# Higher array-use thresholds for side matmuls and zero matmuls, with new order seeds, in a fused transformer-block kernel

## The chip, the cores and the metric

The kernel runs on one core of a Trainium2 chip. The time is device microseconds (us) of one execution. The engines are PE (TensorE matmul; PEld is its weight load), DVE (VectorE), ACT (ScalarE), POOL (GpSimd) and SP (SyncE, which here only issues transfers). PEclk in the profile is the share of full TensorE clock that was granted.

## The reference

One transformer block in bf16: S = 2048 rows, D = 512, 32 heads of 16, hidden width 1376, conditioned by six vectors.

```python
mod = (_silu(c) @ w_mod).reshape(c.shape[0], 6, 1, -1)
sa, ca, ga, sb, cb, gb = ...
h = _layernorm(x) * (1 + ca) + sa
x = x + ga * _A_ref(h, A_wqkv, A_wo)      # softmax attention, 32 heads, Dh = 16
h = _layernorm(x) * (1 + cb) + sb
x = x + gb * _B_ref(h, B_w1, B_b1, B_w2, B_b2)   # gelu(h @ w1 + b1) @ w2 + b2
```

## The kernel before

**Work and tiles.** Attention is cut into 32 runs. A run is four heads for one block of 512 queries (in the last block eight heads for half of it), over 16 key tiles of 128 keys. Each key tile gives four units of 128 x 512 scores: four matmuls that each use 32 of the array's 128 rows (function `qk`, L837). A score unit becomes an exponential in one of two ways. On ACT a group of three or two units goes through Exp (tiles `st` to `pt`, L886). On DVE the four units of a tile are turned into integers that are the bits of an approximate exponential (`ax` to `ph`, L927), and four shifted copies are made (`sh`, L942). A run may give up to four of its 16 tiles to DVE (the first run one); what DVE doesn't get to, ACT takes back (`next_tile`). The product with the values is a group of four matmuls that use 32 columns each (`pv_op`, L975, into `od`); a DVE tile needs five such groups, an ACT tile one. There is one `od` bank, so run follows run. At the end of a run `normalise` copies `od` out and sends the denominators through DRAM on the SP queue, and POOL multiplies (L1027).

**Side work.** All other matmuls run beside attention: projections for queries, keys and values (L716, L755), and for each finished block of 512 rows `block_tail`: output projection (L1135), layer norm, the two MLP matmuls (L1202, L1141). They share the two `ax` PSUM banks with the DVE score units, and DVE evicts most of them. The queries' projections also send 8 small transfers each on the SP queue (`qm<-qs`). A side matmul has a due point, counted in score units done.

**The planner.** Nothing is written out by hand: class `Plan` runs an event model while the program is built, and emits the instructions in the order in which the model starts them. `pick` takes, on each engine, among operations that can start at nearly the same time, the one with the lowest cost (`dyn`, plus `spread`, a pseudo-random 0 to 0.15 made from the kind of the operation and a seed; there is one seed of `SEEDS` for each 25 us of planned time). The order is then fixed; the engines wait on semaphores.

**Array use.** `commit` keeps a list of the array time of the matmuls of the last 30 us (0.2155 us for a full one of 512 columns, a quarter of that for one score unit, `MM`), adds it up backwards, and finds two times, which lie WIN = 3.4 us behind the matmul at which the sum reaches HEAT or FILL. In words: `cool` is when the use of the last 3.4 us falls below HEAT, `fill_at` when it falls below FILL.

```python
            for t, us in reversed(self.done):
                tot += us
                if tot >= HEAT and not self.cool:
                    self.cool = t + WIN
                if tot >= self.fill:
                    self.fill_at = t + WIN
                    break
```

Three rules use them. A side matmul that isn't due yet (`later`) can't start before `fill_at` (`start`, L139). An attention group in `pv_op` that starts after `cool` is doubled: four more matmuls with a zero operand are added to the same bank (`o.extra`, L203, `zeros`, L461). And between operations of PE the planner puts in a single matmul with zeros after `cool` (`heat`, L441 to L455; into a free `ax` bank, L445, or the open `od`, L461) if it ends before the next PE operation can start, or if that is a DVE score unit. Until the first score group (`front`) these zero matmuls don't ask for `cool`.

Of the kernel before, what the change touches and what calls it, by code (L numbers as in the profile page):

```python
# [58 lines left out]
DL = 0.14  # L59
DPL = 0.08  # L60
AL = 0.055
FILL = 1.6
SPREAD = 0.15
SEEDS = (942, 880, 561, 237, 414, 526, 187, 975, 867, 591, 361, 470, 931, 275, 675, 561, 623, 980, 746, 5, 392, 802, 877, 840, 977, 907, 960, 53, 524, 828, 132, 531)
HEAT = 1.45


class Res:
# [38 lines left out]
class Plan:  # L107
    SLACK = {"NIL": 0.0, "PE": 0.10, "DVE": 0.05, "ACT": 0.15, "POOL": 0.05, "SP": 0.05}

    def __init__(self, dyn, later):  # L110
# [6 lines left out]
        self.dve = (0.0, 0.0, True)  # L117
        self.dyn, self.done, self.fill = dyn, deque(), FILL

# [39 lines left out]
    def spread(self, o):  # L159
        x = ((sum(map(ord, o.kind)) if o.eng == "PE" else o.fn.__code__.co_firstlineno if o.fn else 0) * 2654435761 ^ SEEDS[min(int(self.now // 25.0), len(SEEDS) - 1)] * 2246822519) & 0xFFFFFFFF  # L160
        x = ((x ^ x >> 15) * 2246822519) & 0xFFFFFFFF
        return SPREAD * ((x ^ x >> 13) & 1023) / 1024.0
# [33 lines left out]
    def commit(self, s, o):  # L196
# [11 lines left out]
        if o.eng == "PE":  # L208
# [5 lines left out]
# [4 lines that stand above are left out]
# [1250 lines left out]
```

## Time and profile before

| what | before |
|---|---|
| median of 3 runs | 786.5 us (785.47 to 789.52) |
| profiled execution: its time | 786.56 us |
| its span | 784.8 us |
| busy ACT / PE / DVE / POOL | 755.3 / 743.1 / 734.5 / 122.2 us |
| granted clock, mean | 0.995 |

The difference of 1.8 us between time and span lies around the program. Busy times are unions of an engine's instructions. A matmul's recorded duration holds its latency too (a lone group of four takes 0.39 to 0.40 us, two in a row 0.62), so a PE that is busy for 95% of the span isn't at 95% of its throughput. ACT is the busiest, and from 25 to 750 us it hardly pauses. The tables below cut the span into stretches; rows of groups give a line of the kernel, engine, operation, out<-in tiles, shape, count, busy time, mean duration in ns, and the idle time before them.

### The profile page before, as it was taken

What the parts mean: (1) busy time and instruction counts of PE and PEld (TensorE: products, weight loads), DVE (VectorE), ACT (ScalarE), POOL (GpSimd) and SP (SyncE); (2) the same over time, 40 slices, a digit from 0 to 9 for tenths busy, and PEclk for the clock granted to TensorE, in tenths of its full rate; (3) what the DMA queues carried; (4) which work ended last, traced back from release to release, by engine and by line L of the source; (5) the groups of instructions that cost most, each with busy time, mean ns of one, the idle gap of its engine ahead of it and who ended that gap; (6) DMA issues with size and microseconds to landing.
All of it is one profiled execution on the core that took longest, in us unless ns stands there. A gap on an engine that the chain in (4) does not pass through costs nothing.

```text
span 784.8 us, 20739 instructions
## 1 busy us (share of the span) xinstructions
PE 743.1 (95%) x8381; PEld 271.4 (35%) x8381; DVE 734.5 (94%) x1288; ACT 755.3 (96%) x680; POOL 122.2 (16%) x279
## 2 busy tenths in 40 slices
PE   8899999999999998999999999999998999999997
PEld 3433323333333222232223323222243444334445
DVE  6889899999999999999999999999798999999993
ACT  4999999999999999999999999999998999999993
POOL 6520304021122430010000100000000100010100
PEclk9999999999999999999999999999999999999999
DMA  7034011000002010000100110001100001000000
GB/s 215 32 96 129 19 23 47 22 17 20 16 19 71 22 52 18 17 16 22 47 9 20 31 27 26 12 17 30 59 26 18 22 20 46 18 23 18 26 18 28
DMA packets 38545, 27.70 MB, mean 35 GB/s; under 512 B 17941, under 2 KB 33846, under 8 KB 38450
## 3 DMA queue, kind: packets, MB, share of 16 engines
q1 hardware_dynamic: 38442, 26.39, 12.2%
q8 instruction: 65, 1.06, 0.6%
q14 instruction: 30, 0.25, 0.1%
q10 hardware_dynamic: 8, 0.00, 0.0%
HBM read 20.77 MB, written 2.61 MB: 30 GB/s over the span
## 4 chain that ended last, share of the span: by engine, by line
PE 24%; ACT 20%; DVE 13%; issue 5%; DMA 1%; SPq 0%; DVEq 0%; ACTq 0%
ACT pt L886 18%; PE od L975 8%; PE st L837 6%; DVE ph L927 6%; DVE sh L942 4%; PE ax L1141 3%; PE ax L1202 2%; PE ax L837 2%; DVE g L1207 1%; PE ax L716 1%; PE t L1312 1%; ACT g L1217 1%; DVE OD L1000 0%; DMA qm<-qs 0%; DMA dc<-dn 0%
## 5 line engine op out<-in xcount | busy, mean ns | idle before, releaser
L886 ACT ACTIVATE pt<-st 128x1536 bf16<-128x1536 f32 x629 | 714.2, 1312 | 6.0 <-PE st L837 3.8
L927 DVE TENSOR_SCALAR ph<-ax 128x512 int16<-128x512 f32 x476 | 309.8, 684 | 15.2 <-PE ax L837 13.5
L942 DVE TENSOR_SCALAR sh<-ph 128x2048 int16<-128x2048 int16 x476 | 310.1, 695 | 6.1 <-PE od L975 5.7
L837 PE MATMUL st<-qm,kT 32*128 32x512 bf16 x1572 | 247.3, 384 | 20.6 <-ACT pt L886 16.4
L837 PE MATMUL ax<-qm,kT 32*128 32x512 bf16 x476 | 162.1, 380 | 7.3 <-DVE ph L927 3.7
L975 PE MATMUL od<-sh,VX 128*32 128x512 bf16 (+1 forms) x2400 | 166.4, 341 | 2.8 <-DVE sh L942 1.9
L837 PEld LDWEIGHTS <-kT 32*128 32x128 bf16 x2048 | 79.7, 91 | 243.6 <-issue 232.5
L975 PE MATMUL od<-pt,VEB 128*32 128x512 bf16 (+1 forms) x1960 | 144.8, 341 | 0.4 <-ACT pt L886 0.4
L975 PEld LDWEIGHTS <-VEB 128*32 128x32 bf16 x2560 | 62.4, 96 | 72.8 <-issue 59.5
L975 PEld LDWEIGHTS <-VX 128*32 128x32 bf16 x2400 | 58.1, 95 | 84.7 <-issue 73.7
L1027 POOL TENSOR_TENSOR OT<-OD,RB 128x256 bf16<-128x256 f32 x38 | 27.0, 726 | 306.9 <-DVE sh L942 170.2
L975 PE MATMUL od<-ph,VEB 128*32 128x512 bf16 (+1 forms) x600 | 47.6, 338 | 0.7 <-DVE OD L1000 0.6
L1202 PE MATMUL ax<-blk,W 128*128 128x512 bf16 (+1 forms) x176 | 44.7, 356 | 0.6 <-DVE ph L927 0.4
L1027 POOL TENSOR_TENSOR OS<-OD,RB 128x256 bf16<-128x256 f32 x24 | 17.2, 727 | 139.8 <-DVE sh L942 68.3
L716 PE MATMUL ax<-blk,w 128*128 128x512 bf16 x124 | 37.4, 389 | 1.6 <-DVE ph L927 0.6
L1141 PE MATMUL ax<-w,g 128*128 128x512 bf16 x128 | 33.9, 381 | 1.5 <-ACT g L1212 1.0
L771 POOL TENSOR_SCALAR VX<-VEB 128x128 bf16<-128x128 bf16 x64 | 23.2, 362 | 71.7 <-DVE VEB L647 67.8
L1207 DVE TENSOR_SCALAR g<-ax,b1c 128x512 bf16<-128x512 f32 (+1 forms) x44 | 29.4, 678 | 0.1
L621 DVE BATCH_NORM_STATS2 ln_s<-xb 128x6 f32<-128x512 bf16 x32 | 21.7, 677 | 1.3 <-DMA xb<-in_A_x_dram 1.2
L1141 PEld LDWEIGHTS <-g 128*128 128x128 bf16 x176 | 14.2, 97 | 24.0 <-issue 11.1
L1202 PEld LDWEIGHTS <-W 128*128 128x128 bf16 x176 | 13.5, 97 | 23.3 <-issue 18.7
L1000 DVE COPY OD<-od 128x512 f32<-128x512 f32 x31 | 21.3, 686 | 0.1
(106 smaller groups left out, 374.2 us busy)
## 6 DMA issues: line engine op xcount, KB each, us to landing
RB<-rn SPq DMA_DIRECT2D x124, 64.0 KB, 2.1
xb<-in_A_x_dram SPq DMA_DIRECT2D x7, 512.0 KB
out_dram<-o SPq DMA_DIRECT2D x16, 128.0 KB
qm<-qs SPq DMA_DIRECT2D x120, 16.0 KB, 1.8
W<-in_B_w_dram SPq DMA_DIRECT2D x1, 1376.0 KB
w<-in_A_wqkv_dram SPq DMA_DIRECT2D x3, 384.0 KB
blk<-in_w_mod_dram SPq DMA_DIRECT2D x2, 512.0 KB
g<-in_w_mod_dram SPq DMA_DIRECT2D x2, 512.0 KB, 4.3
```

The lines of the kernel that those rows point to most:

```text
L621: nc.vector.bn_stats(out=st6, in_=src)
L716: return chain([(lambda ps, j=j: nc.tensor.matmul(out=ps[:, 0:QB], lhsT=w.tile[:, j, cc * P:(cc + 1) * P], rhs=o_h[b].tile[:, j, :], start ...
L771: nc.gpsimd.tensor_scalar(out=v_cols(VX[(t, ph)])[:, 8 * cc:8 * cc + 8, 0:16], in0=v_cols(v_tile(t, 0))[:, 8 * cc:8 * cc + 8, 0:16], scala ...
L837: nc.tensor.matmul(out=o.tile[:, k * QB:(k + 1) * QB], lhsT=kT[cc][kb][rows, ko * P:(ko + 1) * P], rhs=qm.tile[rows, par, :] if hb is None ...
L886: nc.scalar.activation(out=e.tile[:, 0:len(got) * QB], in_=o.tile[:, 0:len(got) * QB], func=ACT.Exp, scale=ESC)
L927: nc.vector.tensor_scalar(out=ph.tile[:, o.row * QB:(o.row + 1) * QB], in0=o.tile, scalar1=PH_B, scalar2=0.0, op0=ALU.add, op1=ALU.max)
L942: sh = op("DVE", lambda o, j=j: nc.vector.tensor_scalar(out=o.tile, in0=first.tile, scalar1=PH_SH[j], scalar2=None, op0=ALU.add), 0.6, es, ...
L975: nc.tensor.matmul(out=o_od[r].tile[32 * i:32 * i + 32, n * HB:n * HB + w], lhsT=v_tile(kt, ph)[:, c0:c0 + 32], rhs=got[i][:, at:at + w], ...
L1027: two = beside(lambda c: nc.gpsimd.tensor_tensor(out=OT.tile[:, c], in0=OD.tile[:, c], in1=o5.tile[:, c], op=ALU.mult), (OT,), (OD, o5), f ...
L1141: nc.tensor.matmul(out=ps, lhsT=g[:, f, col:col + P], rhs=rhs, start=(f == 0), stop=(f == NF - 1))
L1202: mm = chain([(lambda ps, f=f, j=j, f0=f0: nc.tensor.matmul(out=ps[:, (f - f0) * N:(f - f0 + 1) * N], lhsT=W1[:, j, f * P:(f + 1) * P], rh ...
L1207: ev.append(op("DVE", lambda o, f=f, f0=f0, mm=mm: nc.vector.tensor_scalar(out=g.tile[:, f, 0:N], in0=mm.tile[:, (f - f0) * N:(f - f0 + 1) ...
```

## The change

The two thresholds are raised, FILL from 1.6 to 2.1 and HEAT from 1.45 to 1.7 (us of array time per 3.4 us), and all 32 seeds are replaced. No operation of the block's mathematics changes, and no transfer is added or removed. What changes is the order that the planner emits on every engine, the moment at which side matmuls that aren't due may start, and the number and places of zero matmuls.

```diff
-FILL = 1.6
+FILL = 2.1
 SPREAD = 0.15
-SEEDS = (942, 880, 561, 237, 414, 526, 187, 975, 867, 591, 361, 470, 931, 275, 675, 561, 623, 980, 746, 5, 392, 802, 877, 840, 977, 907, 960, 53, 524, 828, 132, 531)
-HEAT = 1.45
+SEEDS = (189, 218, 297, 155, 171, 163, 261, 540, 974, 172, 672, 279, 663, 728, 301, 465, 719, 329, 508, 485, 116, 24, 319, 395, 351, 431, 815, 192, 264, 111, 379, 921)
+HEAT = 1.7
```

## The prediction

> **What bounds the kernel now.** I read the busy shares first, then the chain that ended last, then the groups, and last the span in stretches of 25 us and, where those looked odd, of 1 us. From the page of the profile:
>
> ```profile
> PE 743.1 (95%) x8381; PEld 271.4 (35%) x8381; DVE 734.5 (94%) x1288; ACT 755.3 (96%) x680; POOL 122.2 (16%) x279
> PE 24%; ACT 20%; DVE 13%; issue 5%; DMA 1%; SPq 0%; DVEq 0%; ACTq 0%
> L886 ACT ACTIVATE pt<-st 128x1536 bf16<-128x1536 f32 x629 | 714.2, 1312 | 6.0 <-PE st L837 3.8
> L927 DVE TENSOR_SCALAR ph<-ax 128x512 int16<-128x512 f32 x476 | 309.8, 684 | 15.2 <-PE ax L837 13.5
> L942 DVE TENSOR_SCALAR sh<-ph 128x2048 int16<-128x2048 int16 x476 | 310.1, 695 | 6.1 <-PE od L975 5.7
> L837 PE MATMUL st<-qm,kT 32*128 32x512 bf16 x1572 | 247.3, 384 | 20.6 <-ACT pt L886 16.4
> ```
>
> ACT, DVE and PE are balanced, and no one of them is the bound alone: the chain changes between them all the time. ACT and DVE share one pool of score tiles. 1572 units on ACT are 393 tiles at 714.2/393 = 1.82 us each; 476 on DVE are 119 tiles at (309.8 + 310.1)/119 = 5.21 us each. Both together do 1/1.82 + 1/5.21 = 0.741 tiles per us. So a microsecond lost on ACT moves the end by (1/1.82)/0.741 = 0.74 us, one lost on DVE by 0.26 us; these are my exchange rates. PE has some room: it waits 16.4 us for ACT to give a score bank back (last row).
>
> The stretches show where ACT doesn't run. Columns: stretch, length, busy time of PE, PEld, DVE, ACT, POOL, granted clock, DMA share, GB/s.
>
> ```profile
> 200.00:225.00 25.00, 24.33 (x248) 8.90 (x246) 23.72 (x41) 24.04 (x22) 5.02 (x11) 0.93 0.08 19
> 575.00:600.00 25.00, 22.57 (x341) 9.09 (x331) 21.21 (x36) 22.32 (x20) 1.40 (x2) 0.93 0.10 27
> ```
>
> ```profile
> 200.00:201.00 1.00, 0.76 (x4) 0.19 (x2) 1.00 (x3) 1.00 (x2) 0.41 (x1) 0.92 0.00 0
> 201.00:202.00 1.00, 1.00 (x5) 0.11 (x3) 1.00 (x3) 1.00 (x2) 0.00 (x0) 0.50 0.00 0
> 203.00:204.00 1.00, 1.00 (x7) 0.24 (x10) 0.13 (x1) 0.95 (x2) 0.00 (x0) 0.50 0.00 0
> 594.00:595.00 1.00, 1.00 (x16) 0.29 (x8) 1.00 (x2) 0.42 (x1) 0.00 (x0) 0.50 0.08 17
> ```
>
> Twice the granted clock falls to half for some 3.4 us, from 200.7 and from 593.3. These are the two stretches before 750 us in which ACT loses the most, 0.96 and 2.68 us; elsewhere it stands for hardly 2 us from 25 to 750.
>
> What PE did ahead of the first of them (timeline):
>
> ```profile
> 198.37 0.37 PE L837 MATMUL ax<-qm,kT 32*128 32x512 bf16 x1
> 199.28 0.40 PE L975 MATMUL od<-pt,VEB 128*32 128x512 bf16 x4
> 199.61 0.39 PE L837 MATMUL ax<-qm,kT 32*128 32x512 bf16 x1
> 199.87 0.39 PE L837 MATMUL st<-qm,kT 32*128 32x512 bf16 x2
> ```
>
> Between 197.4 and 200.7 there are only two attention groups and twelve score units: 2 x 0.2155 + 12 x 0.054 = 1.08 us of array time, while PE was never still for as much as 0.5 us. So in this trace a small sum of array time, not a pause, stands ahead of the half clock.
>
> [...]
>
> **The change, part by part.** The array time of attention alone comes from the groups, shapes kept apart:
>
> ```profile
> L837 PE MATMUL ax<-qm,kT 32*128 32x512 bf16 x476 | 162.1, 380 | 7.3 <-DVE ph L927 3.7 <-DMA qm<-qs 2.0 <-DVE g L1207 0.4
> L975 PE MATMUL od<-sh,VX 128*32 128x512 bf16 x1408 | 123.8, 387 | 2.4 <-DVE sh L942 1.5
> L975 PE MATMUL od<-pt,VEB 128*32 128x512 bf16 x1184 | 108.7, 384 | 0.4 <-ACT pt L886 0.4
> L975 PE MATMUL od<-ph,VEB 128*32 128x512 bf16 x352 | 35.4, 384 | 0.7 <-DVE OD L1000 0.6
> L461 PE MATMUL od<-warm 128*32 128x512 bf16 x208 | 19.2, 392 | 0.0
> L445 PE MATMUL ax<-warm 128*128 128x512 bf16 x24 | 9.5, 471 | 0.0
> ```
>
> Units: 2048 x 0.054 = 110 us. Groups: (1408 + 1184 + 352)/4 = 736 x 0.2155 = 159 us, and the last block's 2016 matmuls of half width another 54 us. Together 323 us over the 742 us from 20 to 762 us in which attention runs: 0.435, or 1.48 us per 3.4 us. So the old HEAT (1.45) lies just below what attention does by itself and the new one (1.7) above it. The side matmuls of that time come to some 114 us by their counts (128 + 132 + 176 + 62 of full width and 108 for the narrow ones by their share, less some 78 at both ends, x 0.2155), 0.52 us per 3.4 us. All work averages 2.0, so FILL at 2.1 lies above the mean: a side matmul that can run will nearly always be let through ahead of its due point.
>
> *Clock.* With more use demanded, the first half-clock stretch should go. Its cost: ACT's 0.96 us and DVE's 1.28 us in that stretch, 0.74 x 0.96 + 0.26 x 1.28 = 1.0 us. The second lies behind a stall from 589 to 592 us, in which PE waited for the query transfers (`qm<-qs`) behind the four `RB` issues on SP's queue; no threshold sees that. Its clock part costs 1.3 us (ACT 1.49, DVE 0.70 from 594 to 596). Bounds: 0 and -2.3. I take -1.0, the one that a low sum alone explains.
>
> *Zero matmuls.* If side work runs at 2.1 - 1.48 = 0.62 us per 3.4 us, its 114 us last 625 of the 742 us; the other 117 us have none. There HEAT asks for 1.7 - 1.48 = 0.22 us, about one group of zeros per 3.4 us: 117/3.4 = 34 groups beside the 52 + 24 that L461 and L445 show now, 7.4 us of PE. Two groups in a row last 0.62 us where one lasts 0.40, so 0.22 us each is right. Cover: PE's 16.4 us of waiting for score banks. Without cover a doubled group holds back the score units queued behind it on PE, and ACT and DVE wait for those. Bounds: 0 if all falls in that wait, 7.4 if none does. I take PE's share of the chain, 24%: +1.8.
>
> *Side work earlier.* It moves DVE's evictions forward too, at the same count. A run takes 742/32 = 23.2 us, four DVE tiles 20.8, so in a run without side work DVE has 2.4 us over that the limit of four tiles leaves unused, while ACT takes back tiles in crowded runs. 117 us are five such runs: 12 us of DVE, 3.1 us of the end. Starting the next run's tiles early softens this (the `sh` copies have four buffers). Against it, DVE is idle 9.8 us from 25 to 125 us, where earlier side work would fit and give back at most 2.5. Bounds: -2.5 and +3.1; I take +1.2, because the evictions that remain after 125 us outweigh those before. The queues: the 8 transfers for each query group go out earlier on SP, which can only move them away from the `RB` issues of a run's end or onto those of another; tail loads and stores find SP free for most of a run, and POOL is busy 16%. These I cost at nothing; SP is the cover, and the 589 us stall shows the price without it: ACT 1.19 and DVE 2.92 us, 1.6 us.
>
> *Seeds.* They reorder operations of nearly the same start. No row prices it. The nearest is the one mishap of this order, the stretch at 575 us: 0.74 x 2.68 + 0.26 x 3.79 = 3.0 us. Bounds: one such mishap less or more, -3.0 and +3.0 (its clock part is in the first term already). I take 0, since an order is only known to have such mishaps, not how many.
>
> The first 20 us don't ask for `cool`, and after 762 us PE is dense: no cost there.
>
> Sum: -1.0 + 1.8 + 1.2 + 0 = +2.0 us on the profiled execution's 786.56 us, 788.56; that one lies 0.06 us above the median of the three runs, so **788.5 us**.
>
> **The rivals.**
>
> *Faster.* Both half-clock stretches go, the query transfers leave early enough that the 589 us stall goes as well, zeros fall in PE's waits, and early side work fills half of DVE's early idle time: -2.3 - 1.6 - 1.3 = -5.2, 781.3 us. The deciding mechanism is the cover: it holds as long as added zeros stay within the 16.4 us in which PE waits for score banks anyway. For it: 7.4 is less than 16.4. Against: those waits are 57 short ones, and the long runs of low use are not where they are.
>
> *Clearly slower.* Zeros lie in PE's path and DVE's evictions bunch: +7.4 + 3.1 - 1.0 = +9.5, 796 us. For it: PE has the largest share of the chain, and DVE is at 24.5 to 25.0 of 25 us in most stretches from 125 to 550 us, so an eviction that comes early pushes a score tile away. It decides where more than some 20 groups are doubled in line.
>
> [...]
>
> *The order hardly differs in what it costs.* If due points and dependences, not `fill_at`, hold most side work back, everything stays within 1 us of 786.5. For it: tail chains wait for each other's evictions.
>
> **How the numbers follow.** The forecast has 0.40 (own range 785 to 792), faster 0.26, clearly slower 0.24, no gain in clock 0.05, no difference 0.05. A measurement of this kernel tells a change from none at about 0.5% (its runs spread 785.47 to 789.52), so the limits are 782.6 and 790.4. Faster keeps its 0.26; slower takes its 0.24 and 0.07 from the upper end of the forecast and the clock case; 0.43 stays between. The range reaches from the faster case with 1.3 us of luck in the seeds, 780, to the slower one, 797.
>
> **What the profile after would show.** The clock term: no stretch with a granted clock of 0.5 around a low sum of array time; if they remain while zeros rise, that step is wrong. Zeros: L461 and L445 with some 30 groups more, and the share of PE in the chain higher. Side work: fewer than 476 units in L927, and DVE idle late in a block. Seeds: other places where ACT stands. The prediction is wrong if ACT's idle time between 25 and 750 us falls below 2 us and L927 keeps its 476 (faster), or if the wait of `pt` L886 for PE rises above 6 us (slower).

## The result and the profile after

The changed kernel takes 783.2 us (median of 6 executions, 782.91 to 783.32); the kernel before, beside it, 787.49 us (785.47 to 789.52). The ratio is 0.9944 (95% interval 0.9925 to 0.9963), 0.6% faster. A second comparison gave 782.8 us and 0.9928 (0.9903 to 0.9952). The forecast was 788.5 us, 2.0 us slower than before; the measured time lies on the other side of the kernel before.

The page of the kernel after (busy shares; the chain that ended last; groups):

```profile
PE 746.6 (96%) x8617; PEld 273.2 (35%) x8617; DVE 737.4 (94%) x1288; ACT 755.3 (97%) x680; POOL 124.5 (16%) x279
PE 34%; DVE 28%; ACT 26%; issue 8%; DMA 2%; SPq 1%; POOL 1%; DVEq 0%; ACTq 0%
L886 ACT ACTIVATE pt<-st 128x1536 bf16<-128x1536 f32 x629 | 714.2, 1308 | 2.2 <-PE st L837 1.0
L927 DVE TENSOR_SCALAR ph<-ax 128x512 int16<-128x512 f32 x476 | 310.4, 682 | 8.0 <-PE ax L837 6.8
L942 DVE TENSOR_SCALAR sh<-ph 128x2048 int16<-128x2048 int16 x476 | 312.6, 694 | 2.1 <-PE od L975 0.9
L837 PE MATMUL st<-qm,kT 32*128 32x512 bf16 x1572 | 246.4, 383 | 16.0 <-ACT pt L886 12.4
L461 PE MATMUL od<-warm 128*32 128x512 bf16 x440 | 41.7, 381 | 0.0
```

ACT's Exp is the same work to a tenth of a microsecond (629 instructions, 714.2 us), and DVE has the same 476 score units, so no tile changed engines. What fell is idle time: ahead of Exp from 6.0 to 2.2 us, ahead of `ph` from 15.2 to 8.0, ahead of `sh` from 6.1 to 2.1. Zero matmuls in `od` rose from 208 to 440, so from 52 groups to 110.

The two stretches in which the kernel before lost the most, in the kernel after (columns as in the prediction: stretch, length, busy time of PE, PEld, DVE, ACT, POOL, granted clock, DMA share, GB/s):

```profile
200.00:225.00 25.00, 23.59 (x272) 8.92 (x264) 25.00 (x42) 25.00 (x23) 6.32 (x12) 1.00 0.10 32
575.00:600.00 25.00, 24.52 (x375) 10.41 (x375) 24.52 (x42) 24.97 (x23) 1.42 (x2) 1.00 0.16 48
```

The clock is full in both, ACT stands for 0.00 and 0.03 us where it stood for 0.96 and 2.68 us (24.04 and 22.32 us busy), and the mean clock of each of the six executions is 1.000 (0.995 in the profiled execution before).

From 25 to 750 us (the first row is the kernel before, the second the kernel after; same columns) ACT is idle for 1.9 us instead of 5.2, and DVE for 22.4 instead of 29.6:

```profile
25.00:750.00 725.00, 691.88 (x7846) 243.92 (x7842) 695.37 (x1200) 719.76 (x626) 103.16 (x207) 1.00 0.11 30
25.00:750.00 725.00, 699.10 (x8139) 247.69 (x8140) 702.63 (x1208) 723.12 (x630) 105.75 (x209) 1.00 0.12 31
```

The prediction had named this as its sign for the faster rival: ACT idle for less than 2 us between 25 and 750 us, with 476 units in L927.

### The profile page after: what moved, and what is told of

It is laid out like the page before. It is cut to its first block, busy times and chain, and to the rows that moved or that the text cites. A ratio compares the mean times of both kernels' runs of the same rounds, so it can differ in the third digit from the quotient of the medians.

```text
span 781.3 us, 21165 instructions
## 1 busy us (share of the span) xinstructions
PE 746.6 (96%) x8617; PEld 273.2 (35%) x8617; DVE 737.4 (94%) x1288; ACT 755.3 (97%) x680; POOL 124.5 (16%) x279
## 4 chain that ended last, share of the span: by engine, by line
PE 34%; DVE 28%; ACT 26%; issue 8%; DMA 2%; SPq 1%; POOL 1%; DVEq 0%; ACTq 0%
ACT pt L886 24%; DVE sh L942 11%; DVE ph L927 11%; PE od L975 11%; PE st L837 10%; PE ax L1141 3%; PE ax L837 3%; PE ax L716 2%; PE ax L1202 2%; PE od L461 1%; DVE OD L1000 1%; DVE ln_s L621 1%; PE ax L1135 1%; DMA xb<-in_A_x_dram 1%; PE ax L755 1%
## 5 line engine op out<-in xcount | busy, mean ns | idle before, releaser
L886 ACT ACTIVATE pt<-st 128x1536 bf16<-128x1536 f32 x629 | 714.2, 1308 | 2.2 <-PE st L837 1.0
L927 DVE TENSOR_SCALAR ph<-ax 128x512 int16<-128x512 f32 x476 | 310.4, 682 | 8.0 <-PE ax L837 6.8
L837 PE MATMUL ax<-qm,kT 32*128 32x512 bf16 x476 | 158.9, 379 | 3.3 <-DVE ph L927 1.6
L837 PEld LDWEIGHTS <-kT 32*128 32x128 bf16 x2048 | 77.2, 91 | 233.6 <-issue 224.3
L975 PE MATMUL od<-pt,VEB 128*32 128x512 bf16 (+1 forms) x1960 | 141.8, 340 | 0.1
L975 PEld LDWEIGHTS <-VX 128*32 128x32 bf16 x2400 | 60.0, 95 | 84.6 <-issue 72.9
L461 PE MATMUL od<-warm 128*32 128x512 bf16 x440 | 41.7, 381 | 0.0
```

Of the source, the lines that this page charges most:

```text
L461: nc.tensor.matmul(out=o_od[r].tile[32 * i:32 * i + 32, :], lhsT=warm[:, 0:32], rhs=warm[:, 0:1].to_broadcast([P, QB]), start=False, stop= ...
L837: nc.tensor.matmul(out=o.tile[:, k * QB:(k + 1) * QB], lhsT=kT[cc][kb][rows, ko * P:(ko + 1) * P], rhs=qm.tile[rows, par, :] if hb is None ...
L886: nc.scalar.activation(out=e.tile[:, 0:len(got) * QB], in_=o.tile[:, 0:len(got) * QB], func=ACT.Exp, scale=ESC)
L927: nc.vector.tensor_scalar(out=ph.tile[:, o.row * QB:(o.row + 1) * QB], in0=o.tile, scalar1=PH_B, scalar2=0.0, op0=ALU.add, op1=ALU.max)
L975: nc.tensor.matmul(out=o_od[r].tile[32 * i:32 * i + 32, n * HB:n * HB + w], lhsT=v_tile(kt, ph)[:, c0:c0 + 32], rhs=got[i][:, at:at + w], ...
```

## The experiments

Each kernel was run several times, and the mean granted clock of each execution was noted. One half-clock stretch of 3.413 us (in the profiled execution of before from 200.84 and from 593.38 us) lowers that mean by 3.413 x 0.5/786 = 0.0022. Two numbers are given below beside the median: the middle clock, and the time "at full clock", which is the median of each execution's time less 0.60 us for each 0.001 of missing clock (the slope comes from the first experiment). The recorded clock is rounded to 0.001 and holds a last stretch after the matmuls have ended (in the trace of before the last matmul ends at 781.2 us, and the clock is at half for the last 0.26 us, from 784.52 us), so this number is good to about a microsecond. On the four chips on which these kernels ran the kernel before came to 783.4, 783.4, 783.7 and 784.0 us at full clock.

### 1. How the executions of before differ

No edit.

> The kernel before, unchanged, to see how its executions differ. Theory clock: the mean granted clock differs between executions in steps of 3.4 x 0.5 / 785 = 0.0022, one step for each half-clock stretch (the profiled one had two, 0.995), and the time rises with the number of steps by 1 to 1.5 us each, from about 784 us at none; executions from 785.5 to 789.5 us have one to four. Theory order: the clock is the same in fast and slow executions, and the spread of 4 us has another source.

In all, 120 executions of the kernel before were compared: median 788.1 us, middle clock 0.993. Their times follow the clock (correlation -0.91), with 0.60 us per 0.001, so 1.3 us for each half-clock stretch, down to 783.7 us at full clock (rows with at least seven executions):

| mean clock | executions | median us |
|---|---|---|
| 0.998 | 7 | 785.2 |
| 0.996 | 11 | 785.9 |
| 0.995 | 14 | 786.8 |
| 0.993 | 31 | 787.5 |
| 0.991 | 35 | 789.0 |
| 0.989 | 9 | 790.8 |

The profiled execution of this run shows why the number differs (stretch 575 to 600 us, and seconds out of it):

```profile
575.00:600.00 25.00, 22.77 (x341) 9.26 (x339) 20.78 (x35) 22.60 (x20) 1.41 (x2) 0.86 0.10 27
592.00:593.00 1.00, 0.79 (x13) 0.24 (x13) 0.88 (x2) 0.78 (x1) 0.00 (x0) 0.99 0.07 17
595.00:596.00 1.00, 1.00 (x15) 0.13 (x7) 0.50 (x1) 0.00 (x0) 0.00 (x0) 0.50 0.00 0
602.00:603.00 1.00, 1.00 (x16) 0.46 (x16) 0.43 (x1) 0.51 (x2) 0.00 (x0) 0.50 0.11 27
```

The same order of instructions had one half-clock stretch after the transfer stall in the execution that the prediction used, and here three in a row, 593.0 to 603.2 us. Its mean clock of 0.991 leaves room for one more (4 x 0.0022 = 0.009). So the theory of the clock holds for the spread of before. The execution of 786.56 us on which the forecast was built was one of its better ones.

### 2. The changed kernel's order without its zeros, and with twice as many

```diff
     def zeros(r):
-        for i in range(4):
+        for i in range(0):            # after_no_zeros
+        for i in (0, 1, 2, 3) * 2:    # after_zeros2
```

The planner doesn't notice: everything else keeps its order.

> The changed kernel's order with the 440 zero matmuls of L461 not emitted; all other instructions and their order stay. Theory clock: by the counts of the trace, windows with an array time under 1.3 us per 3.4 us rise from about 0.4 to 7 or 8 in the loop, so five to eight half-clock stretches per execution, a mean clock of 0.983 to 0.990, and 788 to 793 us with a spread of several us. Theory order (the gain comes from the new seeds' order and the zeros are not needed): 780 to 784 us, as the zeros' 24 us of PE are saved.

> The changed kernel's order with each of the 110 zero groups of L461 emitted twice: 110 x 0.22 = 24 us more of PE, clock already full. Theory that zeros lie in PE's waits (cover): under 2 us slower than the changed kernel, 783 to 785 us. Theory of the prediction's term (PE's share of the chain pays, 24 to 34%): 6 to 8 us, 789 to 791 us.

| zero groups in `od` | executions | median us | clock | at full clock |
|---|---|---|---|---|
| 0 | 12 | 787.4 (785.2 to 792.8) | 0.990 (0.980 to 0.993) | 781.2 |
| 110 | 6 and 10 | 783.2 and 782.8 | 1.000 (one at 0.997) | 783.2 and 782.6 |
| 220 | 5 | 795.5 (794.9 to 796.1) | 1.000 | 794.9 |

Without zeros the stretches are back (clock 0.990 as the theory of the clock had it; the median of 787.4 us is just under its range), in the profiled execution three of them at places where the changed kernel has none:

```profile
325.00:350.00 25.00, 22.89 (x215) 6.92 (x216) 24.22 (x46) 24.38 (x23) 3.28 (x6) 0.93 0.09 26
575.00:600.00 25.00, 23.02 (x346) 9.91 (x347) 23.59 (x40) 23.92 (x22) 1.42 (x2) 0.93 0.13 33
675.00:700.00 25.00, 22.98 (x280) 8.87 (x283) 24.18 (x42) 24.04 (x18) 2.67 (x5) 0.93 0.08 22
```

In this order the zeros buy some 6 us of clock and cost 1.4 to 2 us: 0.02 us per group of 0.22 us. A second group at the same place costs (794.9 - 782.9)/110 = 0.11 us, and there PE takes the chain (kernel with doubled zeros: chain, Exp, zeros):

```profile
PE 45%; ACT 27%; DVE 19%; issue 8%; DMA 1%; SPq 0%; DVEq 0%; POOL 0%; ACTq 0%; POOLq 0%
L886 ACT ACTIVATE pt<-st 128x1536 bf16<-128x1536 f32 x629 | 719.6, 1278 | 9.1 <-PE ax L837 4.2
L461 PE MATMUL od<-warm 128*32 128x512 bf16 x880 | 65.7, 381 | 0.0
```

Both expectations on cost miss: the first 110 groups are nearly hidden, the next 110 cost 12 us, more than the share-of-the-chain rule gave. So, by my reading, cover isn't shared out evenly: a first group mostly finds it, a second one at the same place doesn't.

### 3. The same doubling in the order of before

> The order of before with each of its 52 zero groups of L461 emitted twice (416 matmuls, about as many as the changed kernel). Theory place (zeros help only where the sum is low; these places were already helped): the half-clock stretches stay, clock 0.988 to 0.996, and the time rises by the price of a second group, 0.11 us as measured in the changed kernel's doubling, 52 x 0.11 = 5.8 us: 791 to 796 us. Theory count (so many zeros are enough wherever they are): clock above 0.998, 783 to 787 us.

Median 792.0 us of 8 (791.1 to 794.2), clock 0.996 at best, 789.2 us at full clock. That is 5.5 us over before for 52 groups, again 0.11 us each, though the 104 groups are fewer than the 110 that cost 0.02 us each in the changed kernel: cover seems to be used up place by place, not out of one sum. The profiled execution still has a mean clock of 0.996, as much as two half-clock stretches take (2 x 0.0022). The theory of place holds: as many zeros as in the changed kernel, where zeros were already, don't do what that kernel does. They aren't without effect: the middle clock is 0.996 against 0.993.

### 4. Which zeros

```diff
-            if o.extra:
+            if o.extra and False:           # doubled attention groups left out: after_heat_only
                 zeros(r)
...
-        return Op("PE", lambda o: zeros(r), MM, ...
+        return Op("PE", lambda o: None, MM, ...   # single groups left out: after_extra_only
```

> The changed kernel's order with the zeros of doubled attention groups left out (77 groups); the 33 groups that the planner puts between other work stay (132 matmuls in L461). If the doubled groups guard the clock: three to seven half-clock stretches, clock 0.988 to 0.995, 785 to 790 us. If the planner's own single groups are enough: clock above 0.998 and under 783.2 us, as the doubled ones lie in PE's path.

> The changed kernel's order with the 33 single zero groups left out; the 77 doubled attention groups stay (308 matmuls in L461). Theory clock, by the sum of array time alone: the loss of a third of the zeros leaves one to three half-clock stretches, clock 0.994 to 0.998, 783 to 786 us. If single groups only fill time in which PE stands, the time at full clock is that of the changed kernel, 783 us.

In the third kernel a group is emitted only where the use that was really emitted in the last 3.4 us of planned time is under 1.6 us (`plan.real` holds that use):

```diff
     def zeros(r):
-        for i in range(4):
+        for i in range(4 if needed(plan) else 0):
...
+def needed(plan):
...
+    if sum(u for t, u in plan.real if plan.now - WIN < t < plan.now) >= 1.6:
+        return False
+    plan.real.append((plan.now, 0.2155))
+    return True
```

> The changed kernel's order, but of its 110 zero groups only those are emitted ahead of which the planned use of the last 3.4 us, with what was really emitted, is under 1.6 us (67 groups, 268 matmuls in L461). If a threshold somewhat under 1.7 is enough in this order: clock 0.998 to 1.0 and 782.3 to 783.2 us, faster than both kernels. If not: one to three stretches, 783.5 to 787 us with a spread above 1 us.

| kernel | groups | executions | median us | clock | at full clock |
|---|---|---|---|---|---|
| single groups only | 33 | 6 | 783.1 (782.4 to 786.1) | 0.993 to 1.000 | 782.2 |
| doubled groups only | 77 | 9 | 784.7 (783.4 to 789.3) | 0.990 to 1.000 | 783.3 |
| where under 1.6 us | 67 | 6 | 784.0 (782.5 to 785.3) | 0.995 to 1.000 | 782.7 |

The 33 single groups guard as well as the 77 doubled ones (middle clock 0.998 for both), which is more than I expected. None of the three is enough: stretches come back in some executions, and what is saved at full clock, at most 1 us, is lost there. With six to nine executions no version can be told from the changed kernel as a faster one.

### 5. The three constants one by one

```diff
-FILL = 1.6            # seeds_only: only SEEDS new        fill_only: FILL = 2.1
-HEAT = 1.45           # heat17_fill175: HEAT = 1.7, FILL = 1.75
                       # both_old_seeds: 2.1 and 1.7, old SEEDS
                       # after_heat145: 2.1 and new SEEDS, HEAT 1.45
```

HEAT can't be raised to 1.7 with FILL at 1.6: the loop in `commit` ends at FILL, `cool` would stay 0, and every attention group would be doubled. So HEAT's rise needs FILL's.

> The kernel before with the new seeds alone; FILL 1.6 and HEAT 1.45 stay. Theory clock: zero groups stay near the 52 of before, one to four half-clock stretches per execution, 785 to 790 us, spread of several us. Theory order: 782 to 785 us.

> The kernel before with FILL 2.1 and HEAT 1.7, old seeds. Theory clock: mean clock 0.998 to 1.0 and a spread under 1 us; the time is that of an order without half-clock stretches, some 784 us by the line through the executions of before, plus 1 to 2 us for the zeros, so 783 to 787 us with the chance of the order. Theory seeds (the new seeds are what is worth something): no better than before, 787 to 790 us.

> The kernel before with HEAT 1.7 and FILL only just above it, 1.75, old seeds (FILL must stay above HEAT: the loop in commit ends at FILL and would never set cool). Theory that HEAT alone does it: clock 0.998 to 1.0, 783 to 788 us, about as the one with FILL 2.1. Theory that early side work carries it: half-clock stretches remain, clock 0.990 to 0.996, 786 us and above.

> The kernel before with FILL 2.1 alone, old seeds and HEAT 1.45. Theory that HEAT does it: zeros stay near the 52 groups, two to five half-clock stretches, clock 0.988 to 0.995, 785 to 791 us. Theory of the prediction (evictions bunch): DVE loses tiles to ACT, fewer than 476 units in L927, and DVE's idle time from 25 to 750 us rises above the 30 us of before. Theory early side work: clock near 1.0 and under 785 us.

> The changed kernel with HEAT back at 1.45; new seeds and FILL 2.1 stay. Theory clock: zero groups fall to some 50 to 60, half-clock stretches come back (clock 0.988 to 0.996), 785 to 790 us with a spread of 4 us. Theory order: 781 to 784 us.

| FILL, HEAT, seeds | zero groups in `od` | executions | median us | clock | at full clock |
|---|---|---|---|---|---|
| 1.6, 1.45, old (before) | 52 | 120 | 788.1 | 0.993 | 783.7 |
| 1.6, 1.45, new | 42 | 12 | 789.2 | 0.998 | 787.8 |
| 2.1, 1.45, old | 55 | 8 | 790.9 | 0.997 | 788.7 |
| 1.75, 1.7, old | 97 | 12 | 788.2 | 0.998 | 787.2 |
| 2.1, 1.7, old | 97 | 11 | 790.8 | 0.998 | 789.7 |
| 2.1, 1.45, new | 54 | 12 | 788.2 | 0.998 | 787.3 |
| 2.1, 1.7, new (after) | 110 | 6 and 10 | 783.2 and 782.8 | 1.000 | 783.2 and 782.6 |

Every combination between the two kernels has a better clock than before, and every one is 3.5 to 6 us slower at full clock. Several of these times lie in the expected ranges, but not for the reason given. With HEAT at 1.45 and FILL at 2.1 the clock was expected to be 0.996 or less. It is 0.997 to 0.998 with the 42 to 55 zero groups that the old HEAT gives, just as with the 97 that the new one gives. And with both thresholds and the old seeds the kernel is slower than either theory had it. So the step from 0.993 to 0.998 can't be put down to the thresholds, as each of these other orders brings it; what two raised thresholds are worth by themselves isn't shown. What is shown is that the last step, to 1.000, needs the zeros in the order of the changed kernel (experiment 2).

Any other constant gives the planner another order from some point on. That the two sets of seeds were chosen for their thresholds is my inference, from no other combination being as fast; it fits that each of these orders is then an unchosen one. Where such an order loses is seen in the kernel with both thresholds and old seeds, in DVE's units and in one stretch:

```profile
L927 DVE TENSOR_SCALAR ph<-ax 128x512 int16<-128x512 f32 x464 | 302.3, 681 | 19.8 <-PE ax L837 17.7
300.00:325.00 25.00, 24.42 (x222) 6.93 (x220) 22.03 (x38) 22.16 (x20) 1.41 (x2) 0.87 0.06 15
```

Three tiles fell to ACT (464 units for 476), DVE is idle for 19.8 us ahead of its score units (17.7 us of it until PE has made them), and the granted clock is still only 0.87 in the stretch from 300 us. With FILL alone DVE keeps its 476 units, so the expected bunching isn't seen (its idle time from 25 to 750 us is 32.4 us, where the two profiled executions of before have 29.6 and 32.6), but its idle time ahead of these units is 20.1 us against 15.2 before:

```profile
L927 DVE TENSOR_SCALAR ph<-ax 128x512 int16<-128x512 f32 x476 | 309.0, 681 | 20.1 <-PE ax L837 18.0
```

### 6. What was still open: the stall, and the worth of seeds

The first edit moves the due point of the one query projection whose transfers stood behind the `RB` issues; up to 567 us of planned time the order is that of before. The other two take 32 random seeds, the same for both; the last is the changed kernel again.

```diff
-            due(32 + APR * (first_run(q_made[0]) - 1) - 32)
+            due(32 + APR * (first_run(q_made[0]) - 1) - (48 if q_made[0] == 13 else 32))
```

> The kernel before with the due point of one query projection (group 13, the one whose transfers stood behind the RB issues at 589 us) moved forward by 16 score-unit steps; the planned order is the same up to 567 us of planned time, thresholds and seeds are those of before. Theory that half of before's half-clock stretches come from that transfer stall, which no threshold sees: the stretch at 593 us goes, the median clock rises from 0.993 to 0.996 or more, and the time falls by the stall's 1.6 us and two stretches of 1.35 us, to 783.5 to 785.5 us, unless the new order behind it costs more. Theory thresholds (low sums elsewhere make the stretches): clock 0.993, 786 to 788 us.

> The kernel before (FILL 1.6, HEAT 1.45) with 32 seeds drawn at random. Theory that seeds are worth something only where they were chosen for these thresholds: the line to full clock ends 3 to 6 us above that of before (783.4), at 786.5 to 789.5 us, and the median lies at 788 to 794 us. Theory that seeds are noise of a microsecond or so: full clock 782.5 to 784.5 us.

> The changed kernel (FILL 2.1, HEAT 1.7) with the same 32 random seeds. Theory chosen seeds: full clock 786.5 to 789.5 us, clock 0.997 to 1.0 for most executions, as thresholds keep it up. Theory noise: 782.5 to 784.5 us.

> The changed kernel again, beside the other three on one chip. All executions at clock 0.999 to 1.0 and 782.9 to 783.5 us, if nothing but half-clock stretches spreads the executions of before.

| kernel | zero groups in `od` | executions | median us | clock | at full clock |
|---|---|---|---|---|---|
| before, projection earlier | 45 | 12 | 787.2 (785.2 to 789.6) | 0.998 | 785.7 |
| before, random seeds | 46 | 12 | 789.0 (786.6 to 793.4) | 0.998 | 786.8 |
| after, random seeds | 105 | 12 | 794.3 (792.7 to 797.0) | 0.997 | 792.7 |
| after | 110 | 10 | 782.8 (782.1 to 784.3) | 1.000 | 782.6 |

With the projection earlier, its eight transfers go out 14 us ahead of the `RB` issues (timeline of SP), and the stretch at 593 us is clean, while one between 275 and 300 us (clock 0.93), in the part that keeps the order of before, is left:

```profile
574.24 4.95 SPq L744 DMA_DIRECT2D qm<-qs  x8
588.69 1.71 SPq L1021 DMA_DIRECT2D RB<-rn  x4
```

```profile
275.00:300.00 25.00, 22.09 (x227) 6.58 (x221) 23.18 (x40) 23.53 (x21) 5.49 (x9) 0.93 0.14 40
575.00:600.00 25.00, 23.38 (x353) 10.09 (x353) 24.48 (x42) 24.49 (x23) 1.41 (x2) 1.00 0.19 51
```

The middle clock rises from 0.993 to 0.998, two stretches. So more than half of before's half-clock time seems to hang on that one stall; as the order behind 567 us is another one too, its share isn't separated cleanly. The time gains little: at full clock it is 2 us longer than before, which fits an unchosen order behind 567 us, and the forecast of 783.5 to 785.5 us is missed. This one set of random seeds costs 3 us at the old thresholds, as expected, and 10 us at the new ones, more than expected; where the 10 us are lost wasn't followed. With these seeds, too, the raised thresholds bring no better middle clock. The changed kernel kept its time but not the narrow range that was expected of it: 782.1 to 784.3 us, with one execution at 0.997.

## Why the prediction was wrong

**Two steps failed: the clock by its size, and what was put on the order.** Between the two kernels the clock is worth -4.2 us, where the forecast had -1.0. At full clock they are -0.5 to -1.1 us apart (783.7 against 783.2 and 782.6), where the forecast had +3.0 for zeros, side work and seeds together. The two errors are 3.2 and some 3.5 to 4 us. With either put right alone the forecast would have been a gain, of 1.2 us or of 1.5 to 2.1 us.

**Clock, -1.0 us: too small.** The mechanism was right in that low sums of array time stood ahead of the two half-clock stretches of the profiled execution (1.08 us between 197.4 and 200.7, 0.75 us in the 3.413 us ahead of 593.38), and that the zeros hold the clock in the changed kernel (middle clock 1.000 with them, 0.990 without). But the forecast took one stretch out of one execution. Before has a middle clock of 0.993 where after has 1.000, and 7 x 0.60 = 4.2 us is what this is worth, four times the term and beyond its bound of -2.3. (In the execution on which the forecast was built there were two stretches, 2 x 1.3 = 2.6 us by the same slope.) Two things were missed: the same program has a different mean clock, and so a different number of stretches, from execution to execution (0.982 to 0.998 over the 120; the three times shown, 785.47 to 789.52 us, already had this spread), and the stretch behind the transfer stall, which I left in place, seems to be the one with the most weight. What was put down to the thresholds alone is for the larger part the order: 0.997 to 0.998 came with each of eight other orders that the planner made (experiments 5 and 6), whatever their thresholds. In the changed kernel the transfers of the projection behind the stall leave from 577.5 us, 5 us sooner than before, all eight of them ahead of the `RB` issues, and PE has no such wait. SP before, then after:

```profile
582.86 1.21 SPq L744 DMA_DIRECT2D qm<-qs  x2
584.17 2.95 SPq L1021 DMA_DIRECT2D RB<-rn  x4
587.23 3.67 SPq L744 DMA_DIRECT2D qm<-qs  x6
```

```profile
577.51 1.20 SPq L744 DMA_DIRECT2D qm<-qs  x2
579.42 3.14 SPq L744 DMA_DIRECT2D qm<-qs  x4
583.28 1.14 SPq L744 DMA_DIRECT2D qm<-qs  x2
584.52 1.91 SPq L1021 DMA_DIRECT2D RB<-rn  x4
```

**Zeros, +1.8 us: nearly right, by luck.** All 110 groups together cost 1.4 to 2 us. If the 58 added ones have their share of that, they cost about 1 us (an estimate). The prediction's count of 34 more was short, and its share-of-the-chain price (0.05 us per group) too high for the first groups (0.02 us) and too low for a second group at the same place (0.11 us); the two errors offset each other.

**Side work earlier, +1.2 us: not seen.** The value projections end at 229 us and not 239, the first W1 matmul starts at 356 us and not 361: some 5 to 10 us earlier, where the prediction had side work done 117 us ahead over the whole loop. DVE kept its 476 units, and its idle time from 25 to 750 us fell from 29.6 to 22.4 us. The claim that side matmuls would nearly always be let through fell. In the code zeros count as array use for FILL as well; that they so hold side work back is an argument, and no run shows it.

**Seeds, 0: right as a net, wrong as a reading.** At full clock the two kernels are 0.5 to 1 us apart, zeros included. But behind that stand two large terms: at the old seeds the new thresholds cost 6 us (789.7 for 783.7), and the new seeds give it back. The bound of one mishap, 3 us, was too small for both. How the gain at full clock divides between seeds and side work stays open.

**The sum.** From the median over all executions of before: 788.1 - 4.2 (clock) - 0.5 to 1 (order and zeros) = 782.9 to 783.4, measured 783.2 and 782.8; this is a splitting of the measured times, not a second forecast. The rival called faster, at 781.3 us, had most of the mechanisms: both stretches and the stall gone and zeros at 0.02 us a group. Its last part didn't come: DVE's idle time from 25 to 125 us is 11.2 us in the kernel after and was 9.8 before.

**Idle gaps.** In the profiled execution of before, the 3.413 us ahead of the two half-clock stretches held 1.29 and 0.75 us of array time, counted as in the prediction (1.08 and not 1.29 us without a side matmul that starts 0.07 us ahead of the fall), while PE's longest pause in them was 0.24 and 0.76 us. The same can be counted for every such window from 30 to 760 us in the profiled executions of before and after, 213 in each, as the changes of the clock show where the windows begin (last section); two of those of before are themselves at half clock:

| array time in the window | windows at full clock, before | after | followed by half clock |
|---|---|---|---|
| under 1.0 us | 1 | 0 | 1 |
| 1.0 to 1.2 us | 1 | 0 | 0 |
| 1.2 to 1.36 us | 3 | 0 | 1 |
| 1.36 us and more | 206 | 213 | 0 |

The lowest sum in the kernel after is 1.46 us. In eight windows, three of before and five of after, PE had a pause of 0.53 to 0.67 us and yet a sum of at least 1.36 us, and none was followed by half clock; neither was the one of before from 586.55 us, with a pause of 0.74 us and a sum of 1.35 us. The window ahead of 200.84 us, with no pause above 0.24 us, was. So these counts, and the kernel without zeros (middle clock 0.990), speak against the case of no gain in clock, in which pauses alone lower it.

## What to carry to other kernels

When the granted clock drops for single stretches, as here for 3.413 us at a time, one profiled execution says neither how many there are nor what they cost: take the clock and the time of a dozen executions, fit the one on the other, and compare kernels at full clock and in total. Here the first 110 groups of zero matmuls cost 0.02 us each, and a second group at the same places 0.11 us, half its 0.22 us; that the first ones fell in waits of PE, and that the second ones found that cover used up, is my reading. In a program whose order is planned with seeds, a constant can't be judged with the old seeds alone, as any change gives another order; and a better clock after a change of constants may be the work of that other order.

## What was not expected of the hardware

In the profiled execution of before the granted clock is at half for 3.413 us from 200.84 us and for 3.413 us from 593.38 us. In the execution of experiment 1 it is at half from 592.98 to 603.22 us (0.99 in the second from 592 us, 0.89 in the one from 603 us), 10.24 us and so three times as long, at the same place of the same program. In the trace of before the clock's record begins at 6.28 us, and from there all changes, up and down, to the last at 784.52 us, lie whole multiples of 3.4133 us apart, to within 1 ns: 57, 1, 114, 1 and 55 times. In the trace of the kernel after the record begins at 4.43 us, and the one change, behind the span's end at 782.67 us, lies 228 times 3.4133 us behind it. Counted from the start of the span, the changes lie at other times from one execution to the next: 2.87 us behind multiples of 3.4133 us in before, 2.47 us in the execution of experiment 1, and the two are the same kernel. That a place of low use is therefore divided differently among the windows each time, and that the number of stretches differs between executions for this reason, is my guess; no run shows it.

Ahead of both falls in before the sum was low (1.08 and 0.75 us), but it isn't a sharp limit: a window of the same execution from 566.07 us, counted at 1.19 us, was followed by full clock (some matmul records may be missing there). With the zeros of the changed kernel the spread of the times shrank too: 0.4 us over the first six executions and 2.2 us over the next ten, one of them at 0.997, where before has 4 us over six.
